# Cosine-weighted linear attention and a gated MLP in one kernel: part of v copied beside its ones, a load moved in the program, two token slots turned by DMA

## The chip, the core and the metric

The kernel runs on one core of a Trainium2 chip. A core has TensorE (PE; its weight loads are shown as PEld), VectorE (DVE), ScalarE (ACT), GpSimd (POOL) and SyncE (SP), each with its own stream of instructions, and 16 DMA engines that all of these streams share. The metric is device microseconds of one execution. Before the change it is 296.84 us, the median of 12 runs (295.95 to 298.0).

## What is computed

```python
r = np.maximum(x, 0.0)                                # phi(x), x = q or k: [8, 8, 576, 64]
phi = np.concatenate([r * cos_w, r * sin_w], axis=-1) # 128 features; weights by token position
kv = np.einsum('bhsf,bhsd->bhfd', k_p, v)
z = np.sum(k_p, axis=2)
num = np.einsum('bhsf,bhfd->bhsd', q_p, kv)
den = np.einsum('bhsf,bhf->bhs', q_p, z)[..., None] + 1e-06
attn = num / den
x = attn.transpose(0, 2, 1, 3).reshape(8 * 576, 8 * 64)   # 4608 tokens, 512 wide
h = x @ w_in                                              # to 2048
out = (h * sigmoid(1.702 * h)) @ w_out                    # to 512
```

Eight batches of 576 tokens with eight heads of 64 go through an attention that needs no softmax, and the 4608 tokens then go through a two-layer network.

## The kernel before

The MLP works in nine blocks of 512 tokens (the loop over `i`). A block has 32 slots: slots 0 to 15 are the first layer (`mm1`, one of 16 feature chunks per slot, four matmuls each, then the activation on ScalarE into `g`), slots 16 to 31 the second (`mm2`, four matmuls per slot). The second layer goes through one 128-token tile after the other, except in block 0: there slots 16 to 19 do the first quarter of the sum for all four tiles, slots 20 to 23 the second, and so on, so that slot 24 is the first to read the third quarter of `w_out`, which POOL loads late. Results are copied out of PSUM (`evac`) and stored by POOL.

While block `i` runs, the attention of batch `b = i + 1` is woven in: `at(n, f, ...)` puts a call after the matmuls of slot `n`. The order is thus written out by hand; each engine takes its own instructions in this program order and waits on semaphores for data and for buffers. Inputs are loaded by POOL with a cast to bf16.

For a batch the steps are these. `prep` makes q' and k' (ReLU times cosine or sine) on VectorE. q' (`qn`) has tokens on the partitions and must be turned so that features stand there (`qT`): either `turn_q`, a DMA transpose that SP issues, or `turn_q_at`, eight TensorE transposes into a PSUM tile (`at`, two buffers) and one copy out. Token slots are numbered `c`: four of 128 tokens and a tail of 64. `unit_kv` forms k' times v with a column of ones beside v, which gives z, and copies the result out (`kvs`). `unit_num` forms numerator and denominator of one slot, divides on VectorE, and `turn_x` (DMA) or `turn_x_at` (TensorE) turns the result into `xT`, the input of the first layer.

Batch 0 runs ahead of the loop, by pairs of heads `m`: `kv0(m)` (k' times v), `num0(m)`, `product0(m)` (the division), `turn_x0(m)`, and then the first matmuls of block 0. `kv0` reads v where the load put it: each matmul of it streams 128 columns, 64 of v and, by a stride, 64 of a block of ones that stands after all heads; only 65 of the results are used. Other batches copy v into `vt`, which has a single column of ones per head. In the loop's batch 1, all four whole slots of q' are turned on TensorE: two after slot 22 and two after slot 23, each copied out by ScalarE. `prep` of q' for batch 1 stands at slot 11 (`k0`), k' at slot 20, the copy of v at slot 23, `unit_kv` at slot 24 (`k1`) and the slots' `unit_num` at 25 to 28 (`ks`). From batch 2 on, q' is turned by DMA. In block 0 the SP queue has two DMA transposes: the tail of q' of batch 0 and the tail of its x.

Loads: the start of the program has POOL load batch 0, the weights, batch 1 and batch 2 in one go (lines 125 to 144), each waiting for an earlier one to land. In block `i` from 1 on, `load_all(b + 1)` stands at slot 1, so batch 3 is loaded in block 1. POOL's other instructions are the stores of results, which stand in the second half of each block.

Of the kernel before, what the change touches and what calls it, by code (L numbers as in the profile page):

```python
# [21 lines left out]
def kernel(  # L22
# [9 lines left out]
    nc = tc.nc  # L32
    B, H, S, D = q.shape
# [20 lines left out]
    def rows(c):  # L54
        return 128 if c < 4 else 64

    def wide(b, n):
        return b < 2 and n != "q"

    def krows(b, c):  # L60
        return 96 if b < 2 else rows(c)
# [4 lines left out]
    def mm_tile():  # L66
        return ps.tile([128, TB], F32, name="mm", bufs=4)

    def at_tile():
        return ps.tile([128, 2, 512], F32, name="at", bufs=2)  # L70

    def warmup(n, wps=None):
        wps = at_tile()[:, 0] if wps is None else wps
        for _ in range(n):
            nc.tensor.matmul(wps, warm[:, 0:128], warm, start=True, stop=True)  # L75


    state = {b: {} for b in range(B)}
# [79 lines left out]
    kp = one.tile([128, 6, H, 2 * D], BF16, name="kp")  # L158
    vt = one.tile([128, 6, H, VW], BF16, name="vt")
# [22 lines left out]
    def part(b, n, c, h0, h1):  # L182
        if wide(b, n):
            return state[b][n][:96, 0:48 * D].rearrange("p (h c d) -> p c h d", c=6, d=D)[:, c, h0:h1]
        if c == 4:
            return state[b][n, 4].rearrange("p (h d) -> p h d", d=D)[:, h0:h1]
        return state[b][n][:, 0:32 * D].rearrange("p (h c d) -> p c h d", c=4, d=D)[:, c, h0:h1]
# [7 lines left out]
    def qn_slot(b, c):  # L195

        return state[b]["qn4"] if b < 2 and c == 4 else state[b]["qn"][:rows(c), c]

    def prep(b, n, c, h0=0, h1=H, on=(nc.vector, nc.vector)):
        r = rows(c) if n == "q" else krows(b, c)  # L200
        for cs, w in enumerate((cos6, sin6) if wide(b, n) else (cosw, sinw)):
            o = qn_slot(b, c) if n == "q" else kp[:r, c]
            oc, i, wc = o[:, h0:h1, cs * D:cs * D + D], part(b, n, c, h0, h1), w[:r, c:c + 1]
            if on[cs] is nc.scalar:
                nc.scalar.activation(oc, i, AF.Relu, scale=wc)
            else:
                nc.vector.tensor_scalar(oc, i, 0.0, wc, op0=MAX, op1=MUL)  # L207

    def prep_v_wide(b):
        nc.vector.tensor_copy(vt[:96, :, :, 0:D], state[b]["v"][:96, 0:48 * D].rearrange("p (h c d) -> p c h d", c=6, d=D))  # L210

    def prep_v(b, c, h0=0, h1=H):
        nc.vector.tensor_copy(vt[:krows(b, c), c, h0:h1, 0:D], part(b, "v", c, h0, h1))
# [75 lines left out]
    def mm1(i, fc):  # L289
        hps = mm_tile()  # L290
        if (i, fc) == (1, 0):

            mm1_part(hps, i, fc, 0, 448)
            mm1_part(hps, i, fc, 448, TB)
        else:
            mm1_part(hps, i, fc)
        gelu(hps, fc)
# [17 lines left out]
    def mm2(i, t, part):  # L315

        if part == 0:
            cur[t] = mm_tile()
        yps = cur[t]
        for fc in range(part * 4, part * 4 + 4):  # L320
            nc.tensor.matmul(yps, gT[fc][:, ds(t * 128, 128)], w_out_sb[:, fc, :],  # L321
                             start=(fc == 0), stop=(fc == FC - 1))
        if part == 3 and (i > 0 or t < 3):
            evac(i, t)

    def evac(i, t, on=None):
        ysb = ypool.tile([128, d_model], F32, name="ysb")
        if on is nc.vector:
            nc.vector.tensor_copy(ysb, cur[t])
        else:  # L330
            nc.scalar.copy(ysb, cur[t])  # L331
        for (p0, n, row, step) in pieces(i * 4 + t):
            nc.gpsimd.dma_start(out=out[row:row + (n - 1) * step + 1:step, :], in_=ysb[p0:p0 + n, :])  # L333

    def mm2_last(i, t):

        yps = mm_tile()
        ysb = ypool.tile([128, d_model], F32, name="ysb")
        hd = d_model // 2
        for n in range(2):  # L340
            cols = ds(n * hd, hd)
            if n == 1:
                yps = mm_tile()
            for fc in range(FC):
                nc.tensor.matmul(yps[:, 0:hd], gT[fc][:, ds(t * 128, 128)], w_out_sb[:, fc, cols],  # L345
                                 start=(fc == 0), stop=(fc == FC - 1))
            if n == 0:
                nc.scalar.copy(ysb[:, cols], yps[:, 0:hd])
            else:
                nc.vector.tensor_copy(ysb[:, cols], yps[:, 0:hd])  # L350
            for m, (p0, cnt, row, step) in enumerate(pieces(i * 4 + t)):
                (nc.sync if m == 0 else nc.scalar).dma_start(out=out[row:row + (cnt - 1) * step + 1:step, cols],
                                                             in_=ysb[p0:p0 + cnt, cols])
# [4 lines left out]
    s0 = state[0]  # L358
# [9 lines left out]
    def kv0(m):  # L368

        kv = mm_tile()  # L370
        v3 = s0["v"][:96].rearrange("p (j d) -> p j d", d=D)
        for h in (2 * m, 2 * m + 1):
            for c in range(6):
                j = h * 6 + c
                nc.tensor.matmul(kv[:, ts(h % 2, 128)].rearrange("p (j d) -> p j d", j=2), kp[:96, c, h, :],  # L375
                                 v3[:, j:49:48 - j, :], start=(c == 0), stop=(c == 5))
        o = 2 * m % 4
        nc.scalar.copy(s0["kvs"][:, m // 2, o:o + 2, 0:D + 1], kv[:, 0:256].rearrange("p (h e) -> p h e", e=128)[:, :, 0:D + 1])

    def num0(m):  # L380

# [26 lines left out]
    AC, VE = nc.scalar, nc.vector  # L408
# [15 lines left out]
    for n in range(2):  # L424
        for c in range(6):
            prep(0, "k", c, 4 * n, 4 * n + 4, on=(VE, AC if c > 2 + n else VE))
    warmup(11, mm_tile())
    kv0(0)
    kv0(1)
    num0(0)  # L430
    kv0(2)
    product0(0)
    num0(1)
# [25 lines left out]
    for i in range(NBLK):  # L459
        work = {n: [] for n in range(32)}  # L460
        b = i + 1

        def at(n, f, *a):
            work[n].append(lambda: f(*a))

        if b < B:
            if i == 0:
                at(13, unit_num, 0, 4)
                at(13, turn_x, 0, 4)
            k0, k1, ks = (11, 24, (25, 26, 27, 28)) if i == 0 else (0, 12, (17, 19, 21, 23, 25))  # L470
            at(k0, prep_new, b)
            if i == 1:

                at(2, nc.vector.memset, kp[64:128, 4], 0.0)
                at(2, nc.vector.memset, vt[64:128, 4], 0.0)

                at(0, prep, 1, "q", 4)
                at(0, turn_q, 1, 4)
                at(14, unit_num, 1, 4)
                at(14, turn_x, 1, 4)  # L480
            for c in range(4 if i == 0 else NC):
                at(k0, prep, b, "q", c)
                if i == 0:
                    at(22 + c // 2, turn_q_at, b, c, AC.copy)
                else:
                    at(k0 + c, turn_q, b, c)
            for c in range(6 if b < 2 else NC):
                at(20 if i == 0 else k1 - 4 + c // 2, prep, b, "k", c)
                if b >= 2:
                    at(k1 - 1, prep_v, b, c)  # L490
            if b == 1:
                at(k1 - 1, prep_v_wide, b)
            at(k1, unit_kv, b)
            for c, k in enumerate(ks):
                at(k, unit_num, b, c)
                if i == 0 and c < 4:
                    at(min(k + 2, 31), turn_x_at, b, c)
                else:
                    at(k, turn_x, b, c)
            if 0 < i and b + 1 < B:  # L500
                at(1, load_all, b + 1)
        for n in range(32):
            if n < FC:
                if i > 0 or n > 3:
                    mm1(i, n)
            elif i == 0:
                mm2(i, n % 4, (n - FC) // 4)
            elif i == NBLK - 1 and n >= 28:
                if n == 28:
                    mm2_last(i, 3)  # L510
            else:
                mm2(i, (n - FC) // 4, n % 4)
            for f in work[n]:
                f()
        if i == 0:
            evac(i, 3, nc.vector)
# [30 lines left out]
```

## Time and profile before

| what | value |
|---|---|
| median of 12 runs | 296.84 us |
| the profiled execution | 296.99 us, span 295.0 us |
| PE busy | 285.4 us (97%) |
| DVE, ACT, POOL busy | 105.9, 125.7, 97.9 us |
| DMA | 39.65 MB, mean 134 GB/s |
| chain that ended last | PE 87%, DMA 7%, ACT 2%, DVE 1% |
| DMA pieces on that chain | `qT<-qn` 4%, `v<-in_v_dram` 3% |

The profile is one execution. The span runs from the first to the last instruction. Busy time is the time in which an engine had an instruction under way; matmuls overlap, so PE can be called busy while it is not at its peak. The chain that ended last is followed back from the last instruction: at each step to what released it, or to the instruction before it on its engine. It is the view that says what a saved microsecond is worth. DMA shares over 1 mean that an engine had more than one packet under way.

### The profile page before, as it was taken

What the parts mean: (1) busy time and instruction counts of PE and PEld (TensorE: products, weight loads), DVE (VectorE), ACT (ScalarE), POOL (GpSimd) and SP (SyncE); (2) the same over time, 40 slices, a digit from 0 to 9 for tenths busy, and PEclk for the clock granted to TensorE, in tenths of its full rate; (3) what the DMA queues carried; (4) which work ended last, traced back from release to release, by engine and by line L of the source; (5) the groups of instructions that cost most, each with busy time, mean ns of one, the idle gap of its engine ahead of it and who ended that gap; (6) DMA issues with size and microseconds to landing.
All of it is one profiled execution on the core that took longest, in us unless ns stands there. A gap on an engine that the chain in (4) does not pass through costs nothing.

```text
span 295.0 us, 5047 instructions
## 1 busy us (share of the span) xinstructions
PE 285.4 (97%) x1920; PEld 144.9 (49%) x1956; DVE 105.9 (36%) x355; ACT 125.7 (43%) x214; POOL 97.9 (33%) x117
## 2 busy tenths in 40 slices
PE   8999999999899999999999999999999999999994
PEld 3654465455344554455445544554455444444443
DVE  5850546764480259015901581148114200000000
ACT  6847452653036313641274126511651176126411
POOL 8543370700277026602690268005401200120021
PEclk9999999999999999999999999999999999999998
DMA  7999999999999956996899779946904500011033
GB/s 188 187 204 200 203 198 193 200 129 177 173 189 173 177 118 129 175 179 119 153 185 181 109 139 191 192 91 114 187 8 71 118 36 3 36 71 38 0 71 71
DMA packets 87304, 39.65 MB, mean 134 GB/s; under 512 B 57137, under 2 KB 85041, under 8 KB 87281
## 3 DMA queue, kind: packets, MB, share of 16 engines
q0 software_dynamic: 40848, 27.01, 59.5%
q1 hardware_dynamic: 46272, 12.20, 25.9%
q8 instruction: 15, 0.25, 0.3%
q10 hardware_dynamic: 160, 0.13, 0.2%
q14 instruction: 9, 0.07, 0.1%
HBM read 36.70 MB, written 9.44 MB: 156 GB/s over the span
## 4 chain that ended last, share of the span: by engine, by line
PE 87%; DMA 7%; ACT 2%; DVE 1%; issue 1%; POOL 1%; ACTq 0%; POOLq 0%; DVEq 0%
PE mm L281 39%; PE mm L321 37%; DMA qT<-qn 4%; PE at L265 3%; DMA v<-in_v_dram 3%; PE at L244 3%; PE mm L345 1%; ACT g L286 1%; PE mm L375 1%; PE mm L406 1%; DVE xb L273 1%; ACT qT L226 1%; POOL k L86 0%; PE at L385 0%; ACT xT L402 0%
## 5 line engine op out<-in xcount | busy, mean ns | idle before, releaser
L321 PE MATMUL mm<-w_out_sb,g 128*128 128x512 bf16 x543 | 126.4, 379 | 0.7
L281 PE MATMUL mm<-xT,w_in_sb 128*128 128x512 bf16 x547 | 122.6, 377 | 0.9
L333 POOL DMA_DIRECT2D out_dram<-ysb x54 | 50.7, 943 | 173.1 <-ACT ysb L331 171.6
L286 ACT ACTIVATE g<-mm 128x512 bf16<-128x512 f32 x144 | 85.6, 598 | 45.9 <-PE mm L281 45.4
L281 PEld LDWEIGHTS <-w_in_sb 128*128 128x128 bf16 x564 | 54.4, 98 | 64.3 <-issue 0.3
L321 PEld LDWEIGHTS <-g 128*128 128x128 bf16 x560 | 52.2, 98 | 57.0
L331 ACT COPY ysb<-mm 128x512 f32<-128x512 f32 x34 | 19.9, 586 | 99.4 <-PE mm L321 96.3
L248 DVE CAST kvs<-at 128x260 bf16<-128x260 f32 x14 | 5.4, 426 | 58.2 <-PE at L244 58.2
L273 DVE TENSOR_TENSOR xb<-at,inv 128x512 bf16<-128x512 f32 (+1 forms) x36 | 24.8, 690 | 1.2
L271 DVE TENSOR_SCALAR den<-at 128x8 f32<-128x8 f32 (+1 forms) x36 | 5.9, 165 | 45.5 <-PE at L265 45.5
L350 DVE COPY ysb<-mm 128x256 f32<-128x256 f32 x1 | 0.4, 425 | 59.4 <-PE mm L345 59.4
L265 PEld LDWEIGHTS <-qT 128*128 128x128 bf16 x272 | 12.9, 98 | 10.0 <-DMA qT<-qn 2.3
L207 DVE TENSOR_SCALAR qn<-q,cosw 128x512 bf16<-128x512 bf16 (+1 forms) x36 | 12.7, 359 | 11.4 <-DMA q<-in_q_dram 11.4
L265 PE MATMUL at<-kvs,qT 128*128 128x65 bf16 x272 | 14.2, 194 | 1.9 <-DMA qT<-qn 1.3
L207 DVE TENSOR_SCALAR qn<-q,sinw 128x512 bf16<-128x512 bf16 (+1 forms) x33 | 12.7, 384 | 0.0
L244 PEld LDWEIGHTS <-kp 128*128 128x128 bf16 (+1 forms) x288 | 9.6, 97 | 1.6
L244 PE MATMUL at<-vt,kp 128*128 128x65 bf16 (+1 forms) x288 | 9.8, 193 | 0.0
L86 POOL DMA_DIRECT2D v<-in_v_dram x10 | 8.2, 828 | 2.3 <-DMA w_in_sb<-in_moe_w_in_dram 2.3
L95 POOL DMA_DIRECT2D kt<-in_k_dram x6 | 8.2, 1359 | 1.9 <-DMA k<-in_k_dram 1.9
L86 POOL DMA_DIRECT2D k<-in_k_dram x9 | 7.8, 865 | 2.6 <-ACT g L286 1.9
L207 DVE TENSOR_SCALAR kp<-k,cosw 128x512 bf16<-128x512 bf16 x24 | 8.5, 355 | 0.0
L75 PE MATMUL at<-warm 128*128 128x512 bf16 x18 | 7.1, 548 | 1.2 <-DVE eps L151 1.2
(75 smaller groups left out, 140.3 us busy)
## 6 DMA issues: line engine op xcount, KB each, us to landing
out_dram<-ysb POOLq DMA_DIRECT2D x38, 128.0 KB, 3.0
out_dram<-ysb POOLq DMA_DIRECT2D x16, 256.0 KB, 2.9
q<-in_q_dram POOLq DMA_DIRECT2D x7, 512.0 KB, 9.0
k<-in_k_dram POOLq DMA_DIRECT2D x6, 512.0 KB, 10.9
v<-in_v_dram POOLq DMA_DIRECT2D x6, 512.0 KB, 12.4
w_out_sb<-in_moe_w_out_dram POOLq DMA_DIRECT2D x4, 512.0 KB, 18.0
w_in_sb<-in_moe_w_in_dram POOLq DMA_DIRECT2D x3, 512.0 KB, 11.8
q<-in_q_dram SPq DMA_DIRECT2D x2, 512.0 KB, 4.3
```

What stands on the lines that cost most here:

```text
L75: nc.tensor.matmul(wps, warm[:, 0:128], warm, start=True, stop=True)
L86: on.dma_start(out=state[b][n][:np_, t * D * h0:t * D * h1].rearrange("p (h e) -> p h e", h=h1 - h0), in_=SRC[n][b, h0:h1, 0:np_ * t, :].r ...
L95: on.dma_start(out=t.rearrange("p (h d) -> p h d", h=H), in_=SRC[n][b, :, 512:576, :].rearrange("h p d -> p h d"))
L207: nc.vector.tensor_scalar(oc, i, 0.0, wc, op0=MAX, op1=MUL)
L244: nc.tensor.matmul(kv[:, ds(h % 4 * (D + 1), D + 1)], kp[:r, c, h, :], vt[:r, c, h, 0:D + 1], start=(c == 0), stop=(c == last))
L265: nc.tensor.matmul(nm[:, h // 4, ds(h % 4 * (D + 1), D + 1)], q_slot(b, c)[:, h, :], state[b]["kvs"][:, h // 4, h % 4, 0:D + 1], start=Tru ...
L273: nc.vector.tensor_tensor(state[b]["xb"][:r, c].rearrange("p (n h) d -> p n h d", n=2), nm4[:, :, :, 0:D], inv[:r].unsqueeze(3).to_broadca ...
L281: nc.tensor.matmul(hps[:, c0:c1], w_in_sb[:, kc, ds(fc * 128, 128)], xT[:, kc, ds(i * TB + c0, c1 - c0)], start=(kc == 0), stop=(kc == KC ...
L286: nc.scalar.activation(g, hps, AF.Gelu_apprx_sigmoid)
L321: nc.tensor.matmul(yps, gT[fc][:, ds(t * 128, 128)], w_out_sb[:, fc, :], start=(fc == 0), stop=(fc == FC - 1))
L331: nc.scalar.copy(ysb, cur[t])
L333: nc.gpsimd.dma_start(out=out[row:row + (n - 1) * step + 1:step, :], in_=ysb[p0:p0 + n, :])
```

## The change

Three edits are made. First, in the prologue, two calls of `prep_v_wide` copy v of heads 4 and 5, and 6 and 7, of batch 0 into `vt`, on VectorE after the last k'; `kv0(2)` and `kv0(3)` then stream 65 columns of `vt` in place of 128. Second, in block 0, slots 0 and 1 of q' of batch 1 are turned on TensorE after slot 22, one copied out by ScalarE and one by VectorE; slots 2 and 3 are turned by DMA transposes that SP issues at slot 11. Third, in block 1, the call that loads batch 3 stands at slot 9 in place of slot 1.

```diff
--- before.py
+++ after.py
@@ -206,8 +206,9 @@
             else:
                 nc.vector.tensor_scalar(oc, i, 0.0, wc, op0=MAX, op1=MUL)
 
-    def prep_v_wide(b):
-        nc.vector.tensor_copy(vt[:96, :, :, 0:D], state[b]["v"][:96, 0:48 * D].rearrange("p (h c d) -> p c h d", c=6, d=D))
+    def prep_v_wide(b, h0=0, h1=H):
+        nc.vector.tensor_copy(vt[:96, :, h0:h1, 0:D], state[b]["v"][:96, 6 * D * h0:6 * D * h1]
+                              .rearrange("p (h c d) -> p c h d", c=6, d=D))
 
     def prep_v(b, c, h0=0, h1=H):
         nc.vector.tensor_copy(vt[:krows(b, c), c, h0:h1, 0:D], part(b, "v", c, h0, h1))
@@ -368,14 +369,18 @@
     def kv0(m):
 
         kv = mm_tile()
+        w = 128 if m < 2 else D + 1
         v3 = s0["v"][:96].rearrange("p (j d) -> p j d", d=D)
         for h in (2 * m, 2 * m + 1):
             for c in range(6):
                 j = h * 6 + c
-                nc.tensor.matmul(kv[:, ts(h % 2, 128)].rearrange("p (j d) -> p j d", j=2), kp[:96, c, h, :],
-                                 v3[:, j:49:48 - j, :], start=(c == 0), stop=(c == 5))
+                if m < 2:
+                    o, i = kv[:, ts(h % 2, w)].rearrange("p (j d) -> p j d", j=2), v3[:, j:49:48 - j, :]
+                else:
+                    o, i = kv[:, ts(h % 2, w)], vt[:96, c, h, 0:w]
+                nc.tensor.matmul(o, kp[:96, c, h, :], i, start=(c == 0), stop=(c == 5))
         o = 2 * m % 4
-        nc.scalar.copy(s0["kvs"][:, m // 2, o:o + 2, 0:D + 1], kv[:, 0:256].rearrange("p (h e) -> p h e", e=128)[:, :, 0:D + 1])
+        nc.scalar.copy(s0["kvs"][:, m // 2, o:o + 2, 0:D + 1], kv[:, 0:2 * w].rearrange("p (h e) -> p h e", e=w)[:, :, 0:D + 1])
 
     def num0(m):
 
@@ -424,6 +429,8 @@
     for n in range(2):
         for c in range(6):
             prep(0, "k", c, 4 * n, 4 * n + 4, on=(VE, AC if c > 2 + n else VE))
+    for m in (2, 3):
+        prep_v_wide(0, 2 * m, 2 * m + 2)
     warmup(11, mm_tile())
     kv0(0)
     kv0(1)
@@ -481,7 +488,10 @@
             for c in range(4 if i == 0 else NC):
                 at(k0, prep, b, "q", c)
                 if i == 0:
-                    at(22 + c // 2, turn_q_at, b, c, AC.copy)
+                    if c < 2:
+                        at(22, turn_q_at, b, c, VE.tensor_copy if c % 2 else AC.copy)
+                    else:
+                        at(k0, turn_q, b, c)
                 else:
                     at(k0 + c, turn_q, b, c)
             for c in range(6 if b < 2 else NC):
@@ -498,7 +508,7 @@
                 else:
                     at(k, turn_x, b, c)
             if 0 < i and b + 1 < B:
-                at(1, load_all, b + 1)
+                at(9 if i == 1 else 1, load_all, b + 1)
         for n in range(32):
             if n < FC:
                 if i > 0 or n > 3:
```

## The prediction

> **What bounds the kernel now.** I read the page first, then the chain that ended last in three stretches, then the DMA view and busy time by stretch.
>
> On the page, the busy row of PE in 40 slices and that of the DMA engines:
>
> ```profile
> PE   8999999999899999999999999999999999999994
> DMA  7999999999999956996899779946904500011033
> ```
>
> PE is full in nearly every slice, with dips in the first (loading) and the eleventh (73.8 to 81 us). The 16 DMA engines stand at nine tenths or more from 7 to 103 us. From about 85 us on the chain is PE alone, the same in each block, and no DMA appears on it: the change can act only before that. There the chain has one long DMA piece:
>
> ```profile
> 65.98 0.98 PE mm L281 x4
> 66.97 10.75 DMA qT<-qn
> 77.72 0.04 issue
> 77.77 0.43 PE at L265 x8
> ```
>
> At 77.77 PE takes up token slot 3 of q' of batch 2, which a DMA transpose issued at 66.97 landed at 77.72. PE stood still for it 1.26 us; before that, PE's sequencer shows 0.59 us for slot 2. Everything after 77.77 hangs on this landing: PE being earlier in the prologue or in block 0 is worth nothing if the landing doesn't move with it.
>
> The next two stretches are those that the change edits; first block 0 at slots 16 to 24, then the prologue.
>
> ```profile
> 33.03 6.21 PE mm L321 x28
> 39.24 0.46 PE at L225 x8
> ...
> 39.77 1.94 ACT qT L226 x2
> ...
> 41.75 0.61 PE at L225 x8
> 42.36 0.22 PE mm L321
> ...
> 43.22 1.45 PE at L244 x48
> ```
>
> ```profile
> 14.11 0.67 PE mm L375 x12
> ...
> 15.04 0.67 PE mm L375 x12
> 15.71 0.23 PE at L401 x4
> 15.93 0.22 PE mm L75
> ```
>
> Last, two DMA answers: packets by queue from 61 to 68 us (q0 carries POOL's loads and stores, q1 the transposes from SP), and stretches with the columns DMA share and GB/s at their end.
>
> ```profile
> q0 software_dynamic: 1518, 0.55, 80.7%
> q1 hardware_dynamic: 1487, 0.37, 66.7%
> ```
>
> ```profile
> 42.00:50.00 8.00, 7.62 (x111) 5.01 (x111) 3.94 (x11) 2.63 (x5) 0.20 (x1) 1.00 1.58 191
> 56.00:62.00 6.00, 5.95 (x29) 2.70 (x29) 5.82 (x18) 4.16 (x7) 3.68 (x5) 1.00 1.14 127
> 62.00:77.70 15.70, 14.30 (x126) 7.40 (x126) 6.15 (x20) 5.35 (x9) 1.35 (x3) 1.00 1.47 163
> 84.00:88.00 4.00, 4.00 (x21) 1.76 (x19) 3.58 (x15) 1.78 (x3) 4.00 (x2) 1.00 1.02 192
> ```
>
> [...] 1518 packets of one queue against 1487 of the other while both are full. [...] here the total stays at 163 to 200 GB/s whether one queue runs or two. [...] 12 of 128 columns take 0.67 us (56 ns each), 40 of 65 columns 1.21 us (30 ns).
>
> **The change part by part.** The profiled execution took 296.99 us (span 295.0, 2.0 around it); the median of the 12 runs is 296.84, so I add differences to 296.84.
>
> *Part 1, v of heads 4 to 7 of batch 0 copied beside the ones.* Adds two VectorE copies of 768 elements: from 944 ns for the 3072 of L210 and 282 ns for the 512 of L213, about 0.34 us each. VectorE ends its last k' at 13.29 and next works at 14.15 (`den`, 0.86 us idle). v of heads 4, 5 landed at 12.84 and of 6, 7 at 13.58 (issues from 3.85 and 4.47, 9.0 and 9.1 us), so the copies end by about 13.97 and fit in the gap. Without that cover the 0.7 us would delay `den` and the whole prologue. Removes 63 moving columns from 24 matmuls: 24 x (56 - 30) ns = 0.62 us of PE, behind num0(0). The transposes of x (L401) ran at 15.49, after kv0(3); they also need product 0, which VectorE ends at 15.28. So PE gains 0.2 us here, not 0.6; the rest becomes waiting for VectorE. The copies of xT and the first matmuls follow 0.2 earlier: their weights landed at 14.9 and 16.2, before use.
>
> *Part 2, slots 2 and 3 of q' of batch 1 by DMA.* Removes 16 of 32 transposes on PE and two of four ScalarE copies of 1.03 us; moves one of the remaining two copies to VectorE. From the end of slot 22's matmuls (39.24) to the k'v product (43.22) PE needs 3.98 us: 1.73 of matmul (8 x 0.216), the rest transposes and the waits for the two copies. With one pair of transposes (0.9 us, from 39.07 to the next matmul at 39.97) it needs 2.6: 1.35 less, 1.55 with part 1. But slot 24 reads w_out of group 2, issued at 21.49 and landed 19.7 us later, at 41.2. PE would stand there at 40.7. With the transposes in the DMA queues beside it I put the landing at 41.6. So the k'v product starts at about 42.5 instead of 43.2, a gain of 0.7 for both parts; 1.55 if the weights came first, 0.4 if they landed at 42.0. The VectorE copy of 1024 elements is not in the trace[...].
>
> The two added transposes wait for q' of slots 2 and 3 (34.8 and 35.3 us), and the SP queue puts them ahead of the turn of x of batch 0's tail (36.38), which then waits its turn. A transpose moves 128 x 1024 bf16 = 262 KB; at 192 GB/s alone (84 to 88 us) 1.37 us of DMA each, 2.7 us for two. Earlier ones in this crowd began to move bytes about 3.6 us after issue (the two that landed 7.9 and 6.3 us after issue, 22.43 and 36.38). At one packet for one I put them landing at 44.6 and 48.3, and the tail's x at 49. PE reads slot 2 at 47.5, slot 3 at 49.1 (48.16 and 49.81 less 0.7), the tail's x at 52.5: no stall, but slot 3 has only 0.8 us to spare.
>
> *Part 3, batch 3 loaded at slot 9 of block 1.* The call moves in program order, but POOL issues nothing between slots 1 and 9: in the built program its order, and what it waits for, are the same. Cost and gain nothing; it doesn't do what it says.
>
> *What the 2.7 us of DMA push.* Every POOL load behind 38 us queues behind them: w_out group 3 (44.1, used at 49), q of batch 2 (47.1, used at 53.2), k (51.3, used at 58.4), v (54.4, used at 61): each has over 3 us, so they hide. But the output stores and the loads of batch 3 run on into 57 to 60 us, where six transposes begin (batch 1's tail, then batch 2), whose slot 3 lands at 77.72 with the DMA engines full. If all that landed before slot 3 still does, it lands 2.7 later. Against that: from 56 to 62 us the engines moved 127 GB/s against 163 to 192 elsewhere, room of about 6 x (1 - 127/175) = 1.6 us. I take 2.7 - 1.6 = 1.1 us later, 78.8. PE arrives at 77.77 - 1.3 - 0.7 = 75.7 and stands still for some 3 us where it stood 1.3. Bounds: 2.7 later (no room used) and, with room used in full and the transposes starting 0.7 earlier with the block, 0.8 earlier; 2.0 earlier at most, PE's own arrival.
>
> Sum: prologue -0.2 and block 0 -0.5, both swallowed at 77 us; part 3 zero; landing +1.1. 296.84 + 1.1 = 297.9 us.
>
> **Rivals.** *The room in the queues suffices (faster).* Place: the landing of slot 3 at 77.72. If the pushed-back loads of batch 3 fall behind the transposes instead of among them, the landing follows the block's start, 0.7 us earlier: 296.1 us, at best 294.8. It decides if slot 3 lands before 77.1. For it: 127 GB/s at 56 to 62. Against: one packet for one lets no transpose pass a load, and stores come in between.
> *A wash.* Room and work cancel, landing within 0.6 us of 77.7: 296.8 us.
> *Block 0 stalls too.* If slot 3 of batch 1 lands past 49.1 the gain there is lost, batch 2's transposes start later too; with 1 us late, up to 299.5 us. For it: in block 1 such transposes took up to 13.0 us to land, which from 36 us would be 49. Against: fewer transposes queue here.
>
> **How the numbers follow.** Landing later, 297.9 us: 0.42 (its own range 297.4 to 299.2). Room suffices: 0.32. Wash: 0.14. Block 0 stalls: 0.12. Within 0.2% (0.6 us), about what a measurement of this kernel can tell from no change, lies the wash alone: faster 0.32, same 0.14, slower 0.54. The range 295.5 to 299.6 leaves out the far ends of first and last.
>
> **What would show it.** Right: PE idle for `qT<-qn` near 75.7 to 79 us, longer than 1.3; q1 and q0 sharing the engines from 38 to 48; slot 24 waiting for w_out; POOL's order unchanged. Wrong: the wait at slot 3 of batch 2 gone or shorter (room suffices), or a `qT` wait near 49 us (block 0 stalls); a VectorE gap or wait ahead of `den` would upset part 1.

## The result, and the profile after

The changed kernel takes 300.7 us (median of 8 runs, 299.46 to 302.03) against 296.63 us of the kernel before beside it (32 runs): a ratio of 1.0134, 95% interval 1.0113 to 1.0155, which is 4.1 us slower. The direction was forecast, the size (297.9 us) was not, and 300.7 lies outside the range. The profiled execution took 300.21 us, span 298.2.

First the page of the changed kernel, PE and the DMA engines in 40 slices:

```profile
PE   8889987999699999999999999999999999999994
DMA  7999999999989987999699969975902610011023
```

PE has a new dip in the seventh slice (44.7 to 52.2 us), beside the old one in the eleventh. The chain that ended last names both (start, length, what):

```profile
12.47 1.63 PE mm L381 x24
...
15.57 0.40 PE at L406 x4
...
33.06 4.16 PE mm L322 x19
37.23 14.38 DMA qT<-qn
51.61 0.05 issue
51.65 0.43 PE at L266 x8
...
67.83 0.27 PE mm L282
68.10 12.94 DMA qT<-qn
81.04 0.05 issue
81.08 0.43 PE at L266 x8
```

The kernel before had one DMA piece here, the landing at 77.72. Now there are two: slot 3 of q' of batch 1, turned by the new DMA transpose, lands at 51.61, and slot 3 of batch 2 lands at 81.04. (`unit_num` is L266 here, L265 before; the layers are L282 and L322.) PE's timeline has the length of both standstills at its end, in brackets:

```profile
51.65 0.43 PE L266 MATMUL at<-kvs,qT 128*128 128x65 bf16 x8 [1.88 <-DMA qT<-qn]
...
81.08 0.43 PE L266 MATMUL at<-kvs,qT 128*128 128x65 bf16 x8 [1.96 <-DMA qT<-qn]
```

The list of waits, of the kernel after and then of the one before (us in total, times, longest):

```profile
PE at L266 <- DMA qT<-qn: 4.7, 3, 2.0
PE mm L322 <- DMA w_out_sb<-in_moe_w_out_dram: 1.2, 1, 1.2
```

```profile
PE at L265 <- DMA qT<-qn: 1.3, 1, 1.3
```

Last, busy time by stretch in the kernel after, with granted clock, DMA share and GB/s at the end of each line:

```profile
42.00:50.00 8.00, 7.21 (x98) 4.63 (x99) 3.94 (x11) 1.00 (x2) 0.69 (x1) 1.00 1.48 162
56.00:62.00 6.00, 5.95 (x28) 2.74 (x28) 5.82 (x19) 4.13 (x7) 5.23 (x7) 1.00 1.40 248
62.00:81.00 19.00, 16.14 (x135) 8.20 (x134) 7.70 (x25) 6.55 (x11) 2.32 (x5) 1.00 1.44 168
```

From 42 to 50 us the engines move 162 GB/s where they moved 191: in this stretch, with two transposes beside the loads, they carry less in all. From 56 to 62 us, 248 in place of 127: the pushed-back work did fill the room that the prediction counted on there, and more, as it had taken 175 GB/s as full. (Counted from the start of block 1, which came 1.85 us later, it is 239 GB/s.)

One sum ties this to the time. In seven programs of this study whose chain goes through slot 3 of batch 2, the span less its landing is the same: 295.0 - 77.72 = 217.3 before, 298.2 - 81.04 = 217.2 after. (In an eighth, "part 2 and two idle instructions" below, it is 1.6 us more, with TensorE at half clock, 0.50 granted, for 3.4 us right after the landing.) So the trace's loss of 3.2 us is this landing's 3.3 us, and the question is why it moved by 3.3 and not by the 1.1 of the prediction.

### The profile page after: what moved, and what is told of

It reads as the page before. It is cut to its first block, busy times and chain, and to the rows that moved or that the text cites. A ratio compares the mean times of both kernels' runs of the same rounds, so it can differ in the third digit from the quotient of the medians.

```text
span 298.2 us, 5019 instructions
## 1 busy us (share of the span) xinstructions
PE 283.4 (95%) x1904; PEld 142.9 (48%) x1940; DVE 107.0 (36%) x358; ACT 123.1 (41%) x211; POOL 93.9 (31%) x117
## 4 chain that ended last, share of the span: by engine, by line
PE 83%; DMA 11%; ACT 3%; issue 1%; DVE 1%; SPq 0%; ACTq 0%; DVEq 0%
PE mm L282 38%; PE mm L322 35%; DMA qT<-qn 9%; PE at L266 3%; PE at L245 2%; DMA q<-in_q_dram 2%; PE mm L346 1%; ACT g L287 1%; PE mm L411 1%; ACT qT L367 1%; ACT kp L205 1%; PE mm L381 1%; ACT xT L407 0%; PE at L406 0%; PE at L390 0%
## 5 line engine op out<-in xcount | busy, mean ns | idle before, releaser
L322 PE MATMUL mm<-w_out_sb,g 128*128 128x512 bf16 x543 | 126.4, 379 | 1.9 <-DMA w_out_sb<-in_moe_w_out_dram 1.2
L282 PE MATMUL mm<-xT,w_in_sb 128*128 128x512 bf16 x547 | 122.6, 377 | 0.9
L282 PEld LDWEIGHTS <-w_in_sb 128*128 128x128 bf16 x564 | 54.3, 98 | 64.3 <-issue 0.3
L322 PEld LDWEIGHTS <-g 128*128 128x128 bf16 x560 | 52.2, 98 | 58.6 <-issue 1.5
L266 PEld LDWEIGHTS <-qT 128*128 128x128 bf16 x272 | 12.9, 98 | 13.3 <-DMA qT<-qn 5.9
L266 PE MATMUL at<-kvs,qT 128*128 128x65 bf16 x272 | 14.2, 194 | 5.2 <-DMA qT<-qn 4.7
L207 DVE TENSOR_SCALAR kp<-k,sinw 128x512 bf16<-128x512 bf16 x24 | 8.2, 343 | 0.0
L273 DVE RECIPROCAL inv<-den 128x8 f32<-128x8 f32 (+1 forms) x36 | 7.2, 201 | 1.2
```

What stands on the lines that cost most here:

```text
L266: nc.tensor.matmul(nm[:, h // 4, ds(h % 4 * (D + 1), D + 1)], q_slot(b, c)[:, h, :], state[b]["kvs"][:, h // 4, h % 4, 0:D + 1], start=Tru ...
L273: nc.vector.reciprocal(inv[:r], den[:r])
L282: nc.tensor.matmul(hps[:, c0:c1], w_in_sb[:, kc, ds(fc * 128, 128)], xT[:, kc, ds(i * TB + c0, c1 - c0)], start=(kc == 0), stop=(kc == KC ...
```

## The experiments

The first four divide the change. Their theories: 1, a wait in block 0 plus DMA work pushed into block 1; 2, the DMA work alone sets the late landing; 3, the landing only follows the start of block 1.

**Part 2 alone.** The kernel before, with slots 2 and 3 of batch 1 by DMA:

```diff
-                    at(22 + c // 2, turn_q_at, b, c, AC.copy)
+                    if c < 2:
+                        at(22, turn_q_at, b, c, VE.tensor_copy if c % 2 else AC.copy)
+                    else:
+                        at(k0, turn_q, b, c)
```

> The kernel before with the second edit alone (slots 2 and 3 of batch 1's q' turned by DMA, one copy on VectorE). All three theories: the whole loss is here, +3.3 to +4.2 us over before, with the wait for slot 3 near 50 us (about 1.9) and the one in block 1 near 78 to 81 us. If parts one or three had a share in the loss, it would be under +3.

Measured: 298.34 us, ratio 1.0062 (1.004 to 1.0084), +1.8. A miss: half of the loss. Slot 3 of batch 1 landed at 48.98 and PE read it without a wait; slot 3 of batch 2 landed at 78.61. The other 2.3 us of the loss of 4.1 need part 1 (or part 3).

**Two transposes that nobody reads.** The kernel before, with all four slots on TensorE as it had them, and slots 2 and 3 turned by DMA as well, into a spare tile. This does work that the kernel doesn't need.

```diff
                     at(22 + c // 2, turn_q_at, b, c, AC.copy)
+                    if c >= 2:
+                        at(k0, turn_spare, b, c)
```

`turn_spare` is `turn_q` with another target.

> The kernel before, all four slots turned on TensorE as before, and beside that the same two DMA transposes into a spare tile that nobody reads: the DMA work of the change without its wait. Theory 1 (wait in block 0 plus DMA work pushed into block 1): no qT wait in block 0, landing of batch 2's slot 3 about 1.4 later than before, +1.2 to +2.0 us. Theory 2 (DMA work alone sets the landing at 81): +3.3 to +4. Theory 3 (the landing only follows the start of block 1): 0 within 0.4.

Measured: 299.02 us, ratio 1.0082 (1.0063 to 1.01), +2.5, more than the 1.2 to 2.0 of theory 1 and less than theory 2 wants. PE waits for no `qT` in block 0, and the kernel is slower all the same: the DMA work itself comes out in block 1, where PE waits 3.6 us in all for `qT`. Theory 3 is out. The spare transposes landed at 45.92 and 51.21.

**The changed kernel, slot 3 read later.**

```diff
-            k0, k1, ks = (11, 24, (25, 26, 27, 28)) if i == 0 else (0, 12, (17, 19, 21, 23, 25))
+            k0, k1, ks = (11, 24, (25, 26, 27, 30)) if i == 0 else (0, 12, (17, 19, 21, 23, 25))
```

> The kernel after with unit_num of slot 3 of batch 1 at slot 30 of block 0 in place of 28: the late landing at 51.6 is met by matmuls. The wait of 1.9 us in block 0 shrinks to under 0.5. Theory 1: 1.4 to 2.0 us faster than after, so +2.0 to +2.6 over before. Theory 2: as after, +3.3 to +4. Theory 3: +0.3 to +0.8 (what is left of block 0's wait).

Measured: 298.6 us, ratio 1.0079 (1.0051 to 1.0106): 2.1 us won back with the wait in block 0 gone (1.9 between the two traced executions, 300.21 and 298.29). Slot 3 of batch 1 still landed at 51.38, slot 3 of batch 2 at 79.15. Theory 1 holds, theory 2 does not.

**The changed kernel, slot 3 alone by DMA.**

```diff
-                    if c < 2:
-                        at(22, turn_q_at, b, c, VE.tensor_copy if c % 2 else AC.copy)
+                    if c < 3:
+                        at(22 + c // 2, turn_q_at, b, c, VE.tensor_copy if c % 2 else AC.copy)
```

> The kernel after with slot 3 alone turned by DMA and slots 0 to 2 on TensorE (copies by ScalarE, VectorE, ScalarE). One transpose lands about 10.6 us after issue, near 47, before PE reads it near 49: no wait in block 0. Theory 1: half of the pushed work, +0.5 to +1.0 us over before. Theory 2: +1.6 to +2.0. Theory 3: -0.3 to 0.2.

Measured: 297.6 us, ratio 1.0034 (1.0021 to 1.0047), +1.05. Half the DMA work, no wait for slot 3 in block 0 (landed 46.60), the batch 2 landing at 79.16. That landing is from the slowest of the six executions (298.41 us), so it can't be set against those of the other traces.

So there are two terms, and one riddle: what do parts 1 and 3 add to part 2? Part 3 adds nothing: with the call at slot 1 (the kernel before) the loads of batch 3 were issued from 54.93, 1.82 us after block 1 began, and with the call at slot 9 ("part 1 alone" below) from 54.39, 1.81 us after; POOL and SP have the same instructions in the same order in both traces. For part 1 the timelines gave a clue. Here is VectorE's first instruction of q' of batch 1, in the kernel before, where its load landed at 32.74, and in the kernel after, where it landed at 33.25:

```profile
32.84 0.35 DVE L207 TENSOR_SCALAR qn<-q,cosw 128x512 bf16<-128x512 bf16 x1 [10.43 <-DMA q<-in_q_dram]
```

```profile
33.76 0.35 DVE L207 TENSOR_SCALAR qn<-q,cosw 128x512 bf16<-128x512 bf16 x1 [10.99 <-DMA q<-in_q_dram]
```

It starts 0.5 us after the landing; in the programs without part 1 it was 0.1 us. The waits of these instructions are the same. What differs ahead of them is two more instructions in VectorE's stream, called a shift of 2 below. That the load itself landed 0.5 us later is another matter: in the 14 traces of this study it landed anywhere from 32.63 to 33.50, and the ranges overlap (32.71 to 33.14 with no shift, 32.76 to 33.50 with one of 2).

**Part 2 and two idle instructions.** Part 2 alone, and at the place of part 1 two copies of a single column, into a tile that nobody reads:

```diff
+    for m in (2, 3):
+        nc.vector.tensor_copy(pad[:96, m - 2:m - 1], s0["v"][:96, 12 * D * m:12 * D * m + 1])
     warmup(11, mm_tile())
     kv0(0)
```

> The kernel before with part 2 alone (298.3 us), and beside it two VectorE copies of one column of v each, into a tile that nobody reads, at the place where part 1 copies v of heads 4 to 7. The k'v products stay as before. Part 2 alone turned slot 3 of q' of batch 1 by 49.0 us, all three parts together by 51.6: there VectorE began q' of batch 1 0.5 us after its load landed, and 0.1 us in the programs without part 1. Theory A (two more instructions in VectorE's stream shift its start by that half microsecond, whatever they copy): q' begins 0.5 us after its load, the transposes are issued near 35.8 and 37.1, slot 3 lands at 51 to 52, PE stands still for it 1.5 to 2.0 us in block 0, and the time is 299.7 to 300.8 us. Theory B (it is what part 1 does to PE or to v): as part 2 alone, 297.8 to 298.9 us, slot 3 landed near 49.

Measured: 300.75 us (4 runs, 298.74 to 303.01), ratio 1.0139 (1.0077 to 1.0202); its fastest run lies within those of part 2 alone (297.76 to 298.95). The traced execution is the slowest, 303.01, with two stretches at half clock (0.50 granted, last section). The load landed at 33.27; VectorE's and PE's timelines:

```profile
33.78 0.35 DVE L208 TENSOR_SCALAR qn<-q,cosw 128x512 bf16<-128x512 bf16 x1 [11.49 <-ACT g L287]
...
51.05 0.43 PE L266 MATMUL at<-kvs,qT 128*128 128x65 bf16 x8 [2.02 <-DMA qT<-qn]
```

Two copies of one column bring back the half microsecond, and here also the landing at 51.0 and the wait. What part 1 copies has no share in the late start: theory A. Of the 1.0 us by which the second transpose was issued later than in part 2 alone (37.24 and 36.21), this start is 0.4; the rest is the load, which landed 0.6 later.

**The changed kernel with 14 idle instructions more**, at the head of VectorE's stream:

```diff
+    pad = one.tile([128, 14], BF16, name="pad")
+    for n in range(14):
+        nc.vector.memset(pad[:, n:n + 1], 0.0)
```

> The changed kernel with 14 one-column memsets more at the head of VectorE's stream, while it waits for the first loads, so that VectorE's instructions stand 16 places further on than in the kernel before, in place of 2. Theory A (the place of the instruction in VectorE's stream): if the delay comes at every eighth or sixteenth place, q' of batch 1 begins 0.1 us after its load, slot 3 lands at 49 to 49.5, and the time is 297.8 to 299.2 us. Theory B (what part 1 does to PE or to v): as the changed kernel, 300 to 301.5 us, q' still 0.5 us after its load.

Measured: 298.12 us, ratio 1.0082 (1.0048 to 1.0117). The load landed at 32.64, and VectorE:

```profile
32.73 0.35 DVE L210 TENSOR_SCALAR qn<-q,cosw 128x512 bf16<-128x512 bf16 x1 [10.44 <-ACT g L290]
```

0.1 us again; slot 3 of batch 1 landed at 48.96, slot 3 of batch 2 at 78.45. With the stream shifted by 16 instructions the median is 2.6 us under the changed kernel's, and so is the traced execution (297.59 us against 300.21). But its 13 times fall into two groups, seven from 297.6 to 298.1 us, below all nine of the changed kernel, and six from 300.5 to 301.5, where nothing was won; the trace is the fastest of the first. The second group goes with a lower granted clock (0.994 against 0.997 to 1.0, last section), and whether the transpose missed its time there too is not shown. Nor is all of the trace's gain the shift's: the second transpose was issued 1.1 us earlier than in the changed kernel, 0.4 by VectorE's start and 0.6 by a load that happened to land earlier. In the 14 programs traced, the six with no shift or with one of 16 start 0.1 us after the landing, and the eight with a shift of 2 start 0.5 us after.

Why does a microsecond of later issue cost over two? The DMA view from 48 to 52 us has GB/s in 40 slices of 0.1 us. First the program just above, then the changed kernel:

```profile
GB/s 189 179 179 203 172 195 172 183 179 172 329 143 138 137 154 152 176 189 177 164 28 17 10 8 9 10 10 10 70 124 67 154 138 138 184 184 195 205 200 200
```

```profile
GB/s 200 169 200 169 195 174 195 169 195 174 192 174 178 183 313 148 151 164 147 159 143 135 135 82 15 5 9 10 9 10 12 33 141 191 181 192 184 174 101 97
```

All 16 engines stand nearly still (5 to 33 GB/s) for some 0.8 us at about 50 us. A transpose that is done before it lands at 49.0 to 49.8, one that isn't lands at 51.0 to 51.6, after it (still: under 50 GB/s):

| program | second transpose issued | engines stand still | slot 3 of batch 1 lands |
|---|---|---|---|
| changed, shift of 16 | 36.13 | 50.0 to 50.8 | 48.96 |
| part 2 alone | 36.21 | 50.1 to 50.9 | 48.98 |
| two transposes that nobody reads | 36.51 | 49.6 to 50.5 | 51.21 |
| changed, all mended (below) | 36.83 | 50.6 to 51.4 | 49.82 |
| changed, load held (below) | 36.86 | 49.2 to 50.0 | 51.07 |
| changed, slot 3 read later | 37.04 | 50.1 to 51.0 | 51.38 |
| changed | 37.23 | 50.4 to 51.2 | 51.61 |
| part 2, two idle instructions | 37.24 | 49.8 to 50.6 | 51.01 |

None of the eight lands between 49.9 and 51.0. The issue alone doesn't decide (36.83 was in time, 36.51 was not). What fits all eight is that it matters which comes first, the transpose's end or the stop, whose own start moves from 49.2 to 50.6; no run moved the stop alone, so this is read from the traces and not shown by an experiment. Of the 2.6 us between the landings of part 2 alone and of the changed kernel, 1.0 is the later issue and 0.8 the stop; the rest isn't traced to anything.

**Part 1 alone (part 3 being nothing).** The changed kernel with the line of the kernel before for all four slots:

```diff
-                    if c < 2:
-                        at(22, turn_q_at, b, c, VE.tensor_copy if c % 2 else AC.copy)
-                    else:
-                        at(k0, turn_q, b, c)
+                    at(22 + c // 2, turn_q_at, b, c, AC.copy)
```

> The changed kernel without part 2: all four slots of q' of batch 1 turned on TensorE again. Theory A and the theory of the two landings (everything that part 1 gains before 77 us is swallowed by the landing in block 1): 296.2 to 296.9 us. Theory B (part 1 costs some 2 us in itself): 298.2 to 299 us. If the prologue's 0.2 us carried through: 296.3.

Measured: 297.18 us, ratio 1.000 (0.9976 to 1.0024). Part 1 alone neither gains nor costs. That its 0.2 us are swallowed by the landing in block 1 (78.00, with block 1 begun 0.5 earlier than in the kernel before) and its half microsecond of VectorE is hidden where no DMA transpose hangs on it fits the trace.

**A load that is really later.** The rest asks what the landing in block 1 depends on. Behind a store in POOL's stream, the load of batch 3 must wait for block 1's first results. Here it is combined with part 1 and with all four slots on TensorE, the copies out alternating (against the changed kernel):

```diff
-                    if c < 2:
-                        at(22, turn_q_at, b, c, VE.tensor_copy if c % 2 else AC.copy)
-                    else:
-                        at(k0, turn_q, b, c)
+                    at(22 + c // 2, turn_q_at, b, c, VE.tensor_copy if c % 2 else AC.copy)
...
-                at(9 if i == 1 else 1, load_all, b + 1)
+                at(20 if i == 1 else 1, load_all, b + 1)
```

> Part 1, all four slots of q' of batch 1 turned on TensorE with the copies out alternating between ScalarE and VectorE, and the call that loads batch 3 at slot 20 of block 1, which is behind a store in POOL's stream and so really later. If the bound of the kernel before is the landing of slot 3 of batch 2 in block 1 (PE waits 1.3 us for it and 0.6 for slot 2), the loads of batch 3 no longer run beside those transposes, the wait goes, and the time is 294.5 to 295.5 us. If the landing is set by the transposes themselves: 296.2 to 296.9 us.

Measured: 297.43 us, ratio 1.0023 (0.9999 to 1.0046). A miss, with a reason in the chain (the traced execution is a long one, 300.5 us, with half clock after the standstill, 0.50 granted from 88 to 91 us):

```profile
74.61 1.20 PE mm L322 x6
75.80 11.04 DMA xT<-xb
86.84 0.14 issue
86.98 5.08 PE mm L282 x15
```

Without loads beside them, the six transposes of q' in block 1 landed 2.8 to 4.7 us after issue in place of 5.6 to 13.0 in the kernel before, and no wait for `qT` is left. But the loads, now issued from 74.4 us, run beside the turn of x, and PE stands still 3.2 us for that. So the load has to go between the two.

**The load held to slot 6 of block 1.** The kernel before, and a POOL copy of one column of that slot's activation ahead of the load:

```diff
-                at(1, load_all, b + 1)
+                if i == 1:
+                    at(6, lambda: nc.gpsimd.tensor_copy(gate, gT[6][:, 0:1]))
+                at(6 if i == 1 else 1, load_all, b + 1)
```

> The kernel before, with the load of batch 3 held back in earnest: at slot 6 of block 1 POOL copies one column of that slot's activation into a spare tile, and the call that loads batch 3 comes after it, so that the loads are issued from about 60.5 us in place of 54.9. The order of the waits that this adds is POOL's alone. Theory 1 (the landing of slot 3 of q' of batch 2 is late because the six loads of batch 3 share the engines with the six transposes): the last transpose of the six lands before PE reads it, PE's waits of 1.3 and 0.6 us in block 1 go, and the time is 294.7 to 295.5 us against 296.8. Theory 2 (the work in block 1 is too much for the DMA engines wherever it stands, so that the wait moves to the turn of x): PE waits at the start of block 2 for the turn of x, and the time is 296 to 298 us.

Measured: 295.18 us, ratio 0.9944 (0.9923 to 0.9965), faster than both kernels. Its loads were issued from 61.35 us. Its PE's waits of over 0.2 us:

```profile
PE at L75 <- DVE eps L151: 1.2, 1, 1.2
PE at L226 <- ACT qT L227: 0.3, 1, 0.3
```

No DMA is among them, and on its chain there is none from 12 to 110 us. Theory 1 of this run: the late landing came from six loads and six transposes under way together.

**The changed kernel with the same hold**, the same edit in place of its part 3:

> The changed kernel with the same hold on the load of batch 3. Theory 1: the second of its two waits (2.0 us and some 0.8 us for the slots before, in block 1) goes, the first (1.9 us, slot 3 of batch 1 in block 0) stays: 297.6 to 298.9 us against 300.7. Theory 2: 299.5 to 301 us.

Measured: 296.66 us, ratio 0.9996 (0.9977 to 1.0014). Of the waits for `qT`, that of block 0 is left, alone:

```profile
PE at L267 <- DMA qT<-qn: 2.5, 1, 2.5
...
PE mm L323 <- DMA w_out_sb<-in_moe_w_out_dram: 0.8, 1, 0.8
```

It gained 4.0 us where 2 to 3 were expected (the section on the hardware has a part of the reason). With the hold, the change costs 296.66 - 295.18 = 1.5 us: the wait in block 0 less what it saves there. The other 4.1 - 1.5 = 2.6 us of the loss thus went with the hold. In the four traced executions, none of which shows half clock before the last few microseconds (mean granted clock 0.997 to 1.0), the change costs 300.21 - 296.99 = 3.2 us without the hold and 296.56 - 294.96 = 1.6 with it: so some 1.6 of the 2.6 came through block 1's landing, and about 1 is the clock (last section).

**Everything mended.** The changed kernel with the 14 idle instructions, the hold, and the copy of v of batch 1 ahead of VectorE's copy of q':

```diff
-                at(k1 - 1, prep_v_wide, b)
+                at(k1 - 3, prep_v_wide, b)
```

> The changed kernel with three things mended: 14 one-column memsets at the head of VectorE's stream (q' of batch 1 begins with its load), the load of batch 3 held back to slot 6 of block 1 in earnest, and the copy of v of batch 1 two slots earlier, ahead of VectorE's copy of q'. Theory 1: neither landing is waited for, or slot 3 of batch 1 by less than 0.5 us; block 0 keeps its 0.7 us: 294.0 to 295.3 us. Theory 2: the transposes' 2.7 us of DMA work still come out somewhere: 296.5 to 298 us.

Measured: 296.6 us, ratio 0.9988 (0.9969 to 1.0007). A miss for theory 1, whose range ended at 295.3; theory 2 has it. PE waits for none of the whole slots of q', but 1.4 us for `w_out` in block 0, 1.3 us for the turn of x at the start of block 2, and 0.5 us for the tail of q' of batch 0: the added DMA work comes out at other places. (Its 22 times are spread from 294.6 to 301.9.)

**Part 1, TensorE for all slots, the hold.** The program of "a load that is really later" with the hold in place of slot 20, and the copy of v at `k1 - 3`:

> Part 1, all four slots of q' of batch 1 turned on TensorE with the copies out alternating between ScalarE and VectorE, the copy of v of batch 1 two slots earlier, ahead of these copies, and the load of batch 3 held back to slot 6 of block 1 in earnest. Theory 1: block 1 without its waits (-1.9), block 0 0.4 to 0.7 us shorter: 294.2 to 295.2 us. Theory 2: 296 to 298 us.

Measured: 295.43 us, ratio 0.9958 (0.9943 to 0.9972). Faster than both kernels, but not than the hold alone, and above the 294.2 to 295.2 that were expected: PE waits 1.2 us for VectorE's copy of q', which stands behind k' and v there.

## Why the prediction was right and wrong

- **What bounds the kernel: right.** The end followed slot 3 of batch 2 to 0.2 us in seven programs, and when that wait was taken away, 1.5 us of the 296.65 went with it.
- **Part 1: right in its gain.** From the first k'v product to the first layer's block 0 it took 9.98 us (12.47 to 22.45) in place of 10.18 (12.24 to 22.42), which is the 0.2 us; the nine traces with part 1 have 9.95 on average, the five without 10.13. Block 0 began no earlier for it in this trace, as the k'v product itself began 0.23 later (in the 14 traces it began anywhere from 11.64 to 12.47). The two copies took 0.97 us, not 0.7, and ended at 14.36, 0.03 ahead of `den`: the cover just held. **Wrong in its cost**: two instructions were charged for their own time alone. They also moved the start of q' of batch 1 by 0.4 us, which nothing in the profile of the kernel before could show.
- **Part 2 on PE: nearly void.** `w_out` of group 2 landed at 42.2, not 41.6, and the k'v product started at 43.1 in place of 42.5, where by the same view it had started before (43.06): of 0.7 us, nothing was left. VectorE's copy of 1024 elements out of PSUM, which the trace of the kernel before doesn't have, took 0.68 us, and with the 0.94 us copy of v behind it VectorE was done at 41.95, 1.1 us ahead of the k'v product: it cost PE nothing.
- **The step that failed** is "At one packet for one I put them landing at 44.6 and 48.3 ... no stall, but slot 3 has only 0.8 us to spare". They landed at 46.5 and 51.6, and the second came 1.9 us after PE was ready. Of its 3.3 us, 1.9 are in the issue: 37.23 where the step had 35.3. Some 0.9 of that is there in part 2 alone too (36.21): one transpose holds SP's sequencer for 1.2 us (35.90 to 37.13 for the first one here), which the step left out for the second. Another 0.5 is the load, which landed that much later in this execution, and 0.4 is VectorE's start. The other 1.4 us are a longer way from issue to landing, 14.4 in place of 13.0, of which the stop of the engines took 0.8; how the step got its 13.0 from the packets is not written out. So the rival "block 0 stalls too", given 0.12, came about. It was priced at up to 299.5 us for a landing 1 us past 49.1; it landed 2.5 us past it, and the profiled execution took 300.21. What the runs of the changed kernel lose by the clock, nearly 1 us in the median, had no term in the prediction.
- **The pushed landing: right where nothing else came in.** Predicted 78.8; part 2 alone landed at 78.61, the program with a shift of 16 at 78.45, and both took 298.1 to 298.3 us in the median against the forecast's 297.9. Both traces are the fastest execution of their program, so the closeness of the landings is in part luck. And the sum behind it, 2.7 us of work less 1.6 of room, is not borne out: with part 2 alone the engines moved 258 GB/s from 56 to 62 us where the sum had 175, which is 0.79 MB more than before and thus more than the 0.52 MB of both transposes; the landing came later all the same. In the changed kernel block 1 began 1.85 us later, and the landing followed by that and more, to 81.04.
- **Part 3: right.** The call moved, the program didn't. The prediction could have gone on from there: a load that really moves is worth 1.5 us.

## What to carry to other kernels

Give a transfer that others wait for a margin in microseconds before trusting it to a full DMA queue: here 0.8 us on paper did not cover a queue that issues one transpose after the other (0.9 us), a load that landed 0.5 us later and another engine's instruction that began 0.4 us later. Before moving work to the DMA engines, ask which transfers run beside the last one that is waited for; here holding six loads back by 6 us won 1.5 us, where none of the three edits won anything in the time. And check in the built program whether a moved call has moved: POOL had nothing between the two places, and the loads went out 1.81 us after block 1 began in place of 1.82; behind a copy that waits for slot 6's activation they went out at 61.35 us in place of 54.93.

## What the runs showed of the hardware

**A full stop of the DMA engines.** In each of the eight programs with two added transposes, the engines stood at under 50 GB/s for 0.8 to 0.9 us at about 50 us, beginning 0.8 to 1.0 us after a transfer of 16 KB of instructions started (at 49.4 in the changed kernel, where it took 0.97). In the kernel before and in the one with the hold, where no transpose is under way from 48 to 52 us, the rate stays at 164 to 237 GB/s. With one added transpose, which had landed with the tail's x by 47.4, before the 16 KB transfer at 48.5, it stays at 150 or more. The kernel before has such a stop from 64.5 to 65.6 us, again with transposes under way and a 16 KB transfer at 63.4. That the transfer or the transposes cause it is not shown.

**The place of an instruction.** A shift of two in VectorE's stream made it start 0.5 us after its semaphore's event in place of 0.1, in every trace; a shift of 16 did not. In the late case it starts together with POOL's next load (33.76 and 33.78 in the changed kernel), in the other 0.43 us ahead of it. The wait itself is not late: the trace has its end 0.05 us after the load's landing in all 14 programs (33.30 in the changed kernel, 32.79 before), so the 0.4 us lie between the end of the wait and the next instruction. What fills them stays open.

**Half clock after a wait of 2 us.** In the trace of "part 2, two idle instructions", PE stood still from 49.0 to 51.05; stretches after that, with the granted clock third from the end of each line:

```profile
52.00:53.00 1.00, 1.00 (x5) 0.45 (x4) 0.65 (x1) 0.00 (x0) 0.00 (x0) 0.50 1.45 198
53.00:54.00 1.00, 1.00 (x6) 0.52 (x5) 0.00 (x0) 0.97 (x2) 0.09 (x1) 0.50 1.83 175
...
55.00:56.00 1.00, 1.00 (x9) 0.56 (x8) 0.00 (x0) 0.85 (x2) 0.00 (x0) 1.00 1.46 200
```

Half speed from 51.55 us for some 3.4 us, which costs 1.7 us. The clock went to 0.50 twice more, for 3.4 us each time: from 82.27, as a wait of 2.3 us ended (PE went on at 82.31), and in the program with the load at slot 20 from 88.0, 1.0 us after a wait of 3.2 us had ended at 86.98. The length of the wait is not all: after the waits of 1.88 and 1.96 us in the changed kernel's trace the granted clock stayed at 1.00, and so it did after the wait of 2.5 us in the changed kernel with the load held (1.00 from 51 to 80 us). What else decides is not shown. One such dip is 0.6% of the span (1.7 of 298 us): seven of the nine executions of the changed kernel had a mean clock of 0.994 (300.4 to 302.0 us), the two at 0.998 and 0.999 took 299.5 and 300.2. So by an estimate from these nine, nearly 1 us of its 4.1 is the clock's, and a wait of 2 us can cost nearly 4. With the hold, 13 of the 14 executions of the changed kernel had 0.997 or more, so the clock's share was won back too, as part of the 4.0 us there.
